# Retention over the flat row of all tokens: 36 whole chunks instead of 40 chunks with half ones

## The chip, the cores and the metric

The kernel runs on one core of a Trainium2 chip. The metric is the device time of one execution in microseconds (us); lower is better. The core has a matrix engine (TensorE, PE in the profile, with PEld for its weight loads), VectorE (DVE), ScalarE (ACT), GpSimd (POOL) and SyncE (SP), which issues most DMAs.

## The reference, cut to what matters

Two stages. The first is retention: for each of 8 sequences and 8 heads, causal scores weighted with a power of a decay, times v. The second is a feed-forward layer with a squared ReLU. All is fp32.

```python
batch, n_heads, seq, head_dim = (8, 8, 576, 64)      # q, k, v
scores = (1.0 / np.sqrt(D_)) * np.matmul(q, k.transpose(0, 1, 3, 2))
gamma = 1.0 - 2.0 ** (-5.0 - np.arange(H))
Dmat = np.where(rel >= 0, gamma[:, None, None] ** rel[None, :, :], 0.0)   # rel = i - j
x = np.matmul(scores * Dmat, v)                      # then to (4608 tokens, 512)
h = np.maximum(x @ w_in, 0.0)                        # w_in (512, 2048)
out = h * h @ w_out                                  # w_out (2048, 512)
```

A sequence has 576 tokens: four and a half times 128, or nine halves of 64. The rows of x are the tokens of sequence 0, then of sequence 1, and so on: a flat row of 4608 tokens, which is 36 times 128.

## The kernel before

**Retention in chunks.** The scores are not formed over whole sequences. Tokens are taken in chunks of 128, each of two halves of 64 (`C`, `CH`). The decay is split into a factor on q (`scale_q`, L374) and one on v (`scale_v`, L488), both from the table `dv`, so that a plain causal mask is left. For a half chunk of 64 tokens, `own_of` multiplies the masked scores with v; the influence of all earlier halves comes through a state of 64 x 64 per head, which `grow_of` sums up in PSUM (`u_ps`), `grown` copies to SBUF (`u_sb`), and TensorE multiplies with q (the loops at L518 and L645: "reads of the state"). The first half of a sequence reads no state, the last grows none. All matmuls here are 64 x 64; the two heads of a pair sit on different halves of the array.

**Chunks of a sequence.** The list `chunks` (L91) starts anew with each sequence: four chunks of 128 tokens and one of 64, 40 in all. For the half one, `cs` is 64: its instructions work on 64 of the 128 partitions, `retain_a` returns at once, and `grow_of` of its second half is left out.

**Three forms.** Chunks 0 to 3 are worked on whole (`scores_full`, `retain_full`). Chunks 4 to 9 are turned by TensorE (`turn_in`, L431) and worked on in three pieces (`retain_a`, `retain_b`, `retain_c`) between steps of the feed-forward layer. From chunk 10 on (`N_TURN` is 11, `N_ONE` 10), q and k are turned by VectorE (`flip`, L399) and moved to their place by ScalarE in 16 small copies per chunk (`move`, L414), and `whole` (L624) does one chunk's retention in one block:

```python
out_of, into = own_of(i, 0, 1), grow_of(i, 1) if more else []
m = beside_each(out_of, into, (0, 2))[-1]
...
grows = i + 1 < N_CH and chunks[i + 1][3] == C
out_of, into = own_of(i, 1, 1) if cs == C else [], grow_of(i + 1, 0) if grows else []
beside_each(out_of, into, (0, 2))
```

`beside_each` issues two own products, then two growing products, in turn: own products of one half take one half of the array's rows, growing products of the next half the other. `whole` also makes the scores of the next chunk (L472) and masks them on VectorE (`masked`, L484). `wait_for` puts a nop on TensorE that waits for an earlier matmul.

**The feed-forward layer.** It goes in 9 blocks of 512 tokens (`TOK`). Block 0's first product (`first_in`, L716, 16 steps) is computed while the weights are converted by VectorE in small pieces (`round_parts`, L212 to L230). For the other blocks, `ffn_in` makes the first product in 28 steps each, four groups of seven products (a Strassen-like scheme, `PRODUCTS`, kept in three PSUM banks h_a, h_b, h_c in the order a b c a b c b). A step is 4 matmuls (L752) and what follows on ScalarE (L762, L768), VectorE (L764, L766, L771, L775, L778, the square L759, the sums L693 and L694) or GpSimd (the square L769). The conversion of w_out (`w_out_parts`) and the sums of x (`sum_x`, L676 to L679) fill VectorE in the same steps.

**The order** is written out by hand (L894 to L993): for each chunk its block, the loads of a later one, then some steps. How many steps is set in `ffn` (L839) from the tokens gone by (`PACE`). SP issues the loads in that order (`load`, L133): two DMAs for q, two for k, one for v. When retention is over (about 507 us) the rest of the first product follows, and from 561 us on the second product (`inner`, L1094), which retention does not touch.

Of the kernel before, what the change touches and what calls it, by code (L numbers as in the profile page):

```python
# [40 lines left out]
def kernel(  # L41
# [48 lines left out]
    NCH = -(-S // C)  # L90
    chunks = [(b, ci, ci * C, min(C, S - ci * C)) for b in range(B) for ci in range(NCH)]  # L91
    N_CH = len(chunks)
# [40 lines left out]
    def load(i, names="qkv"):  # L133
        b, ci, c0, cs = chunks[i]
        if i == 0:
            nc.sync.dma_start(dv, decays)
        got = loaded.setdefault(i, [None] * 3)
        for name, pool, src in (("q", ld3, q), ("k", ld5, k), ("v", ld4, v)):
            if name not in names:
                continue  # L140
            t = got["qkv".index(name)] = pool.tile([128, H, D], F32, tag=name, name=f"{name}_ld")

            issue = nc.scalar if i == 0 and name != "q" else nc.sync
            at = src[b, :, c0:c0 + cs, :].rearrange("h s d -> s h d")
            if name == "v":
                issue.dma_start(t[:cs], at)
            else:

                for e in range(2):
                    issue.dma_start(t[:cs, e * HP:(e + 1) * HP, :], at[:, e::2, :])  # L150
# [167 lines left out]
    dv = only.tile([128, H, 2 * NCH], F32, name="dv")  # L318
# [55 lines left out]
    def scale_q(i, engine):  # L374
        ci, cs = chunks[i][1], chunks[i][3]
        t = loaded[i][0][:cs]
        engine.tensor_tensor(t, t, dv[:cs, :, NCH + ci:NCH + ci + 1].to_broadcast([cs, H, D]), op=ALU.mult)  # L377

# [3 lines left out]
    N_TURN = 11  # L382
# [11 lines left out]
    def flip(i):  # L394
        cs = chunks[i][3]
        t = work2.tile([128, 4, 2, HP, 32], F32, tag="flip", name="flip")

        def one(j):
            nc.vector.transpose(t[:cs, :, j, :, :], loaded[i][j][:cs].rearrange("s (p e) (d a) -> s (e d) p a", e=2, d=2))  # L399

        def two():
            one(0)
            to = new_qk(i)
            for b in range(cs // 32):
                for g in range(4):

                    moves.append((i, done[0] + 2, to[32 * g:32 * g + 32, :, :, 32 * b:32 * b + 32], t[32 * b:32 * b + 32, g, :, :, :]))

        flips.extend([lambda: one(1), two])
# [7 lines left out]
    def turn_in(i, js=(1, 0)):  # L417

        cs = chunks[i][3]
        n_h = cs // CH  # L420
        if "p" not in st[i]:
            if i < N_EARLY:
                p = [ps_e.tile([128, 512], F32, tag=f"e{h}", name="t_ps") for h in range(2)]
            else:
                t = ps_t[0].tile([128, 2, 512], F32, tag="t", name="t_ps")
                p = [t[:, h, :] for h in range(2)]
            st[i]["p"] = [x.rearrange("p (j d t) -> p j d t", j=2, d=HP) for x in p]
        for j in js:
            for hp in range(HP):
                for h in range(n_h):  # L430
                    nc.tensor.transpose(st[i]["p"][h][:, j, hp, :], loaded[i][j][rows(h), 2 * hp:2 * hp + 2, :],  # L431
                                        ident[rows(h), rows(h)])

    def turn_out(i, engines=(0, 1)):

        n_h = chunks[i][3] // CH
        p = st[i].pop("p")
        to = new_qk(i)
        copies = (nc.scalar.copy, nc.vector.tensor_copy)
        if n_h == 2:  # L440
            for h in range(2):
                copies[engines[h]](to[:, :, :, CH * h:CH * h + CH], p[h])
        else:
            for j in (1, 0):
                copies[1 - j](to[:, j, :, 0:CH], p[0][:, j, :, :])
# [5 lines left out]
    def scores(i, part=False):  # L451

        b_, ci, c0, cs = chunks[i]
        if i < N_EARLY:

            sc = [ps_f.tile([128, 512], F32, tag="f", name="sc_ps")[:, 0:256].rearrange("p (h t) -> p h t", h=HP) for e in range(2)]
        else:
            both = ps_t[0].tile([128, 2, 512], F32, tag="t", name="sc_ps")[:, :, 0:256].rearrange("p e (h t) -> p e h t", h=HP)
            sc = [both[:, e, :, :] for e in range(2)]
        st[i]["sc"] = sc  # L460
        st[i]["both"] = None if i < N_EARLY else both
        if part:
            return
        for hp in range(HP):
            score(i, hp)
        masked(i)

    def score(i, hp):
        for h in range(chunks[i][3] // CH):
            for e in range(2):  # L470
                t = slice(CH * h, CH * h + CH)
                nc.tensor.matmul(st[i]["sc"][e][rows(h), hp, :], lhsT=st[i]["kT"][rows(e), hp, t], rhs=st[i]["qT"][rows(e), hp, t],  # L472
                                 start=True, stop=True, skip_group_check=True)

    def masked(i):

        b_, ci, c0, cs = chunks[i]
        sc, both = st[i]["sc"], st[i]["both"]
        r = st[i]["ret"] = st[i]["kT"].rearrange("p (e a) (b t) -> p e (a b) t", e=2, b=2)
        if i < N_EARLY:  # L480
            for e in range(2):
                nc.vector.tensor_tensor(r[:cs, e, :, :], sc[e][:cs], msk[:cs, 0, :, :].to_broadcast([cs, HP, CH]), op=ALU.mult)
        else:
            nc.vector.tensor_tensor(r[:cs], both[:cs], msk[:cs].to_broadcast([cs, 2, HP, CH]), op=ALU.mult)  # L484
# [3 lines left out]
    def scale_v(i):  # L488
        ci, cs = chunks[i][1], chunks[i][3]
        vs = st[i]["vs"] = loaded[i][2]  # L490
        nc.gpsimd.tensor_tensor(vs[:cs], vs[:cs],  # L491
                                dv[:cs, :, ci:ci + 1].to_broadcast([cs, H, D]), op=ALU.mult)
# [4 lines left out]
    def grown(i, h):  # L497
        nc.scalar.copy(u_sb[(2 * chunks[i][1] + h + 1) % 3], u_ps[0])

    def retain_a(i):  # L500

        b_, ci, c0, cs = chunks[i]
        xp[0] = ps_x.tile([128, 2, 256], F32, tag="x", name="x_ps", padded_shape=[128, 2, 512])
        clean.clear()
        if cs < C:
            return
        beside_each(own_of(i, 1, 1), grow_of(i, 0), range(0, H, 2))
        grown(i, 0)

    def retain_b(i):  # L510

        s = st[i]
        b_, ci, c0, cs = chunks[i]
        for h in reversed(range(cs // CH)):
            if 2 * ci + h == 0:
                continue
            u = u_sb[(2 * ci + h) % 3]
# [5 lines left out]
    def retain_c(i):  # L523

        b_, ci, c0, cs = chunks[i]
        more = ci + 1 < NCH
        own, grow = own_of(i, 0, 0), grow_of(i, 1) if more else []
# [3 lines left out]
        x_out(i, lambda: grown(i, 1) if more else None)  # L531
# [17 lines left out]
    def carry_full(i):  # L549
# [3 lines left out]
        if chunks[i][1] == 0:  # L553
            u_ps[0] = ps_u.tile([128, HP, D], F32, tag="u", name="u_ps")
            return
        u = u_sb[2 * chunks[i][1] % 3]
# [4 lines left out]
    def retain_full(i):  # L561

        ci = chunks[i][1]
# [3 lines left out]
        for hp, e, b in HEADS:  # L567
            nc.tensor.matmul(u_ps[0][rows(e), hp, :], lhsT=loaded[i][1][:, 2 * hp + e, :], rhs=st[i]["vs"][:, head(hp, e), :],
                             start=(ci == 0 and hp == 0), stop=(hp == HP - 1), skip_group_check=True)
        x_out(i, lambda: grown(i, 1))  # L570

    def x_out(i, after):

        b_, ci, c0, cs = chunks[i]
        tok = b_ * S + c0
        at = tok
        p = xp[0][:, :, 0:256].rearrange("p a (g t) -> p a g t", g=2)
        while at < tok + cs:
            n = at // TOK

            while steps and steps[0][0] <= n - 2:
                if i >= N_ONE:
                    move(2)
                step()
            end = min(tok + cs, (n + 1) * TOK)
            nc.scalar.copy(xT[n][:, :, at - n * TOK:end - n * TOK].rearrange("p (g a) t -> p a g t", a=2),
                           p[:, :, :, at - tok:end - tok])
            if at == tok:
                after()
            at = end  # L590
            if n_next[0] < N_BLK and (n_next[0] + 1) * TOK <= at:
                steps.extend(block_steps(n_next[0]))
                n_next[0] += 1
        st[i] = loaded[i] = None


    def grow_of(i, h):

        ci = chunks[i][1]
        if ci == 0 and h == 0:  # L600
# [4 lines left out]
            start=(ci == 0 and h == 0 and hp == 0), stop=(hp == HP - 1), skip_group_check=True) for hp, e, b in HEADS]  # L605
# [18 lines left out]
    def whole(i):  # L624

        b_, ci, c0, cs = chunks[i]
# [3 lines left out]
        more = ci + 1 < NCH  # L630
        out_of, into = own_of(i, 0, 1), grow_of(i, 1) if more else []
        m = beside_each(out_of, into, (0, 2))[-1]
        beside_each(out_of, into, (4, 6))
        if more:
# [6 lines left out]
        for h in range(cs // CH):  # L641
            if 2 * ci + h == 0:
                continue
            u = u_sb[(2 * ci + h) % 3]
# [3 lines left out]
        grows = i + 1 < N_CH and chunks[i + 1][3] == C  # L648
        out_of, into = own_of(i, 1, 1) if cs == C else [], grow_of(i + 1, 0) if grows else []
# [5 lines left out]
        if cs == C:  # L655
            wait_for(m)
        beside_each(out_of, into, (4, 6))
        x_out(i, lambda: grown(i + 1, 0) if grows else None)
# [180 lines left out]
    def ffn(i, half):  # L839

        gone[0] += chunks[max(0, min(i, N_CH - 1))][3] / 2
        if half == 2:
            gone[0] += chunks[min(i + 1, N_CH - 1)][3] / 2
# [110 lines left out]
    for i in range(N_EARLY + 1, N_CH + 1):  # L954
# [9 lines left out]
        else:  # L964
# [11 lines left out]
            if i == N_ONE:  # L976
# [3 lines left out]
                grown(i, 0)  # L980
# [220 lines left out]
def _decays(B, H, S, D):  # L1201
# [4 lines left out]
    n = -(-S // C)  # L1206
    s = np.arange(n * C).reshape(n, C)
# [37 lines left out]
```

## Time and profile before

| | us |
|---|---|
| three executions | 961.95, 962.40, 962.91 (median 962.4) |
| the execution profiled | 962.51, span of its trace 960.6 |
| first retention block in one piece | from 121.07 |
| last retention block | from 506.56 |
| second product begins | about 561 |

| engine | busy share of the span from 100 to 508 us |
|---|---|
| TensorE | 404.0 of 408 us |
| VectorE | 350.1 |
| ScalarE | 255.6 |
| GpSimd | 100.6 |

In a list of groups a row names the line, the engine, the operation, what is written and read, the shape (partitions x elements) and the count, then total busy time, mean ns of one, and the engine's idle time just before them with what ended it. In a timeline a row has start and length in us. In a list of waits the numbers are total, times and longest. TensorE's records of one fp32 matmul come in twos, so that a step of 4 matmuls shows as x8.

### The profile page before, as it was taken

The numbers are of one execution on the slowest core, as the hardware profiler recorded it, in microseconds if no ns is written. First come the engines' busy times: TensorE is split into PE (matmuls) and PEld (weight loads), VectorE is DVE, ScalarE is ACT, GpSimd is POOL, SyncE is SP. The second block draws the span as 40 slices with busy tenths as digits, with TensorE's granted clock in tenths as the row PEclk, the third lists the DMA queues.
The fourth block names the chain that finished last, engine by engine and source line by source line (L and its number), as shares of the span: only waits on it lengthen the run. The fifth ranks groups of instructions, "written<-read, shape, count | busy, mean of one in ns | idle before, by whom it ended". The sixth has DMA issues, their size and how long they took to land. (4 is left out here: it accounts for less than half of the span.)

```text
span 960.6 us, 23424 instructions
## 1 busy us (share of the span) xinstructions
PE 945.7 (98%) x9750; PEld 848.6 (88%) x9750; DVE 787.7 (82%) x1446; ACT 337.3 (35%) x807; POOL 135.4 (14%) x123
## 2 busy tenths in 40 slices
PE   8999999999999999999999999999999999999998
PEld 6654788888888888888888899999999999999998
DVE  5889799879799797987966588888888787787876
ACT  3444485856756766757520010000000000000000
POOL 4312132223213213212110000000000000000000
PEclk9999999999999999999999999999999999999999
DMA  9985666767667756765259985435444454524251
GB/s 228 258 242 120 172 187 179 202 221 214 180 170 234 232 166 177 253 177 151 95 221 351 363 277 205 160 138 187 149 171 176 170 190 156 198 100 176 89 176 44
DMA packets 172778, 181.40 MB, mean 189 GB/s; under 512 B 118912, under 2 KB 133248, under 8 KB 166016
## 3 DMA queue, kind: packets, MB, share of 16 engines
q1 hardware_dynamic: 170576, 179.38, 59.5%
q8 instruction: 76, 1.25, 0.6%
q10 hardware_dynamic: 2096, 0.52, 0.2%
q14 instruction: 30, 0.25, 0.1%
HBM read 109.36 MB, written 70.52 MB: 187 GB/s over the span
## 5 line engine op out<-in xcount | busy, mean ns | idle before, releaser
L752 PE MATMUL h_b<-room,w 128*128 128x256 f32 x768 | 183.6, 382 | 2.1 <-DVE room L771 1.8
L414 ACT COPY qk<-flip 32x256 f32<-32x256 f32 x416 | 167.4, 402 | 6.1
L752 PEld LDWEIGHTS h_b<-room,w 128*128 128x128 f32 x768 | 144.1, 190 | 23.9 <-DVE room L771 3.2
L1094 PE MATMUL o_b<-w,room 128*128 128x128 f32 x1168 | 144.4, 275 | 0.2 <-DVE room L1046 0.2
L1094 PEld LDWEIGHTS o_b<-w,room 128*128 128x128 f32 x1168 | 137.3, 192 | 0.4 <-DVE room L1046 0.4
L752 PE MATMUL h_a<-room,w 128*128 128x256 f32 x512 | 122.0, 381 | 1.8 <-issue 1.8
L1094 PE MATMUL o_c<-w,room 128*128 128x128 f32 x1008 | 123.0, 275 | 0.0
L752 PE MATMUL h_c<-room,w 128*128 128x256 f32 x512 | 121.7, 380 | 0.0
L1094 PEld LDWEIGHTS o_c<-w,room 128*128 128x128 f32 x1008 | 117.7, 192 | 0.0
L752 PEld LDWEIGHTS h_a<-room,w 128*128 128x128 f32 x512 | 96.4, 190 | 15.1 <-issue 1.7
L1108 ACT COPY r<-o_a 128x128 f32<-128x128 f32 x53 | 14.1, 266 | 271.6 <-PE o_a L1094 235.9
L752 PEld LDWEIGHTS h_c<-room,w 128*128 128x128 f32 x512 | 96.7, 190 | 13.3
L1094 PE MATMUL o_a<-w,a 128*128 128x128 f32 x688 | 85.6, 275 | 0.0
L769 POOL TENSOR_TENSOR room<-room 128x512 f32<-128x512 f32 x32 | 35.9, 1121 | 335.9 <-ACT room L768 299.4
L1094 PEld LDWEIGHTS o_a<-w,a 128*128 128x128 f32 x688 | 81.2, 192 | 0.1
L759 DVE SCALAR_TENSOR_TENSOR room<-room 128x512 f32<-128x512 f32 x96 | 70.7, 736 | 3.3
L716 PE MATMUL h_ps<-room,w 128*128 128x512 f32 (+2 forms) x160 | 59.6, 518 | 3.5 <-DVE w L230 2.2
L377 POOL TENSOR_TENSOR q_ld<-q_ld,dv 128x512 f32<-128x512 f32 (+1 forms) x39 | 46.2, 1185 | 80.6 <-DMA q_ld<-in_q_dram 76.1
L491 POOL TENSOR_TENSOR v_ld<-v_ld,dv 128x512 f32<-128x512 f32 (+1 forms) x40 | 53.9, 1349 | 7.0 <-DMA v_ld<-in_v_dram 7.0
L716 PEld LDWEIGHTS h_ps<-room,w 128*128 128x128 f32 x160 | 26.8, 190 | 27.4 <-issue 20.7
L609 PEld LDWEIGHTS x_ps<-qk,v_ld 64*64 64x64 f32 x1024 | 38.8, 134 | 13.0 <-issue 11.6
L771 DVE TENSOR_TENSOR room<-h_b,room 128x512 f32<-128x512 f32 x32 | 21.9, 684 | 33.5 <-PE h_b L752 33.5
(115 smaller groups left out, 1377.1 us busy)
## 6 DMA issues: line engine op xcount, KB each, us to landing
g_dram<-room SPq DMA_DIRECT2D x164, 256.0 KB, 3.9
a<-g_dram SPq DMA_DIRECT2D x30, 1024.0 KB, 5.8
room<-g_dram SPq DMA_DIRECT2D x15, 1024.0 KB, 5.9
w<-w_dram SPq DMA_DIRECT2D x7, 1792.0 KB, 10.7
out_dram<-room SPq DMA_DIRECT2D x17, 512.0 KB, 3.3
q_ld<-in_q_dram SPq DMA_DIRECT2D x64, 128.0 KB, 4.1
w<-in_moe_w_in_dram SPq DMA_DIRECT2D x16, 512.0 KB, 6.4
w<-in_moe_w_out_dram SPq DMA_DIRECT2D x16, 512.0 KB, 4.2
```

The costliest lines, as they stand in the source:

```text
L377: engine.tensor_tensor(t, t, dv[:cs, :, NCH + ci:NCH + ci + 1].to_broadcast([cs, H, D]), op=ALU.mult)
L414: nc.scalar.copy(*moves.pop(0)[2:])
L491: nc.gpsimd.tensor_tensor(vs[:cs], vs[:cs], dv[:cs, :, ci:ci + 1].to_broadcast([cs, H, D]), op=ALU.mult)
L609: return [lambda hp=hp, e=e, b=b: nc.tensor.matmul(x_at(hp, e, b, h), lhsT=s["vs"][rows(h), head(hp, e), :], rhs=s["ret"][rows(h), e, hp, ...
L716: nc.tensor.matmul(p, lhsT=w[:, c, :], rhs=xT[0][:, c, :].rearrange("p (h t) -> p h t", h=2)[:, lo:hi, at[0]:at[1]], start=(c == 0), stop= ...
L752: nc.tensor.matmul(p[:, mm, :], lhsT=w[:, c, :], rhs=xs[n][right][:, c, :], start=(j in OPENS and mm == 0 and c == 0), stop=(j in CLOSES a ...
L759: nc.vector.scalar_tensor_tensor(t, t, 0.0, t, op0=ALU.max, op1=ALU.mult)
L769: nc.gpsimd.tensor_tensor(g["A11"], g["A11"], g["A11"], op=ALU.mult)
L771: nc.vector.tensor_tensor(g["A22"], p, p15, op=ALU.add)
L1094: nc.tensor.matmul(p, lhsT=s["lefts"][left][:, m, :], rhs=w_out[j][:, m, WO_SLOT[right], :], start=(i in OPENS and m == 0), stop=(i in CLO ...
L1108: nc.scalar.copy(r[:, 0, 0:128], p)
```

## The change

The chunks no longer start anew with a sequence. There are `n_tok // C` = 36 of them, all of 128 tokens, along the flat row; the half with number `2 * i + h` has the position `(2 * i + h) % 9` in its sequence. Two sequences take nine chunks; in the fifth of them, the first half is the end of one sequence and the second half the start of the next. Which half reads and grows a state is decided by half. The loads of such a chunk are two for each one of another chunk, with 64 rows each. The decay table has nine patterns of chunks instead of five, and goes from 80 to 144 columns. The three forms change over at chunk 9 instead of 10 (`N_TURN` 10), which is the same token. Before the reads of a state beside which no state was grown, `retain_b` waits for the products before. `x_out` no longer splits a chunk at a block's border. The diff, cut to its core:

```diff
-    NCH = -(-S // C)
-    chunks = [(b, ci, ci * C, min(C, S - ci * C)) for b in range(B) for ci in range(NCH)]
-    N_CH = len(chunks)
+    N_CH = n_tok // C
+    N_SEQ = S // CH
+    N_PAT = decays.shape[2] // 2
+
+    def pos(i, h):
+        return (2 * i + h) % N_SEQ
+
+    def grows(i, h):
+        return i < N_CH and pos(i, h) < N_SEQ - 1
...
+            b, c0 = divmod(i * C, S)
+            runs = [(b, c0, slice(0, C))] if c0 + C <= S else [(b, c0, slice(0, CH)), (b + 1, 0, slice(CH, C))]
+            for e in range(1 if name == "v" else 2):
+                for b, c0, to in runs:
...
-    dv = only.tile([128, H, 2 * NCH], F32, name="dv")
+    dv = only.tile([128, H, 2 * N_PAT], F32, name="dv")
...
-    N_TURN = 11
+    N_TURN = 10
...
-        if cs < C:
-            return
-        beside_each(own_of(i, 1, 1), grow_of(i, 0), range(0, H, 2))
-        grown(i, 0)
+        st[i]["made"] = beside_each(own_of(i, 1, 1), grow_of(i, 0), range(0, H, 2))[-1]
+        if grows(i, 0):
+            grown(i, 0)
...
-        for h in reversed(range(cs // CH)):
-            if 2 * ci + h == 0:
+        if not grows(i, 0):
+            wait_for(s["made"])
+        for h in (1, 0):
+            if pos(i, h) == 0:
                 continue
-            u = u_sb[(2 * ci + h) % 3]
+            u = u_sb[(2 * i + h) % 3]
...
-        ci = chunks[i][1]
-        if ci == 0 and h == 0:
+        if not grows(i, h):
+            return []
+        begins = pos(i, h) == 0
+        if begins:
             u_ps[0] = ps_u.tile([128, HP, D], F32, tag="u", name="u_ps")
...
-        grows = i + 1 < N_CH and chunks[i + 1][3] == C
-        out_of, into = own_of(i, 1, 1) if cs == C else [], grow_of(i + 1, 0) if grows else []
+        out_of, into = own_of(i, 1, 1), grow_of(i + 1, 0)
         beside_each(out_of, into, (0, 2))
...
-        gone[0] += chunks[max(0, min(i, N_CH - 1))][3] / 2
-        if half == 2:
-            gone[0] += chunks[min(i + 1, N_CH - 1)][3] / 2
+        gone[0] += C if half == 2 else C / 2
...
-    n = -(-S // C)
-    s = np.arange(n * C).reshape(n, C)
+    half = np.arange(2 * (S // CH)) % (S // CH)
+    s = (half[:, None] * CH + np.arange(CH)).reshape(-1, C)
```

## The prediction

> **What bounds the kernel now.** I read the engine shares first. TensorE is busy for 98% of the span; VectorE follows with 82%.
>
> ```profile
> span 960.6 us, 23424 instructions
> PE 945.7 (98%) x9750; PEld 848.6 (88%) x9750; DVE 787.7 (82%) x1446; ACT 337.3 (35%) x807; POOL 135.4 (14%) x123
> ```
>
> TensorE is the bound nearly everywhere, so a change is worth what it takes from TensorE's own sequence, or from the 15 us in which TensorE idles. The list of waits, cut to PE, says what those are:
>
> ```profile
> PE h_ps L716 <- DVE w L230: 2.2, 3, 1.6
> PE h_a L752 <- issue: 1.8, 1, 1.8
> PE h_b L752 <- DVE room L771: 1.8, 2, 1.3
> ```
>
> About 5.4 us of idle lie in the first 40 us and 2.6 at the end; the middle has these three lines: weights that VectorE converts (40 to 100 us), one idle without visible cause at 411.9, and a PSUM bank that VectorE must read before the sixth product of a step group goes into it.
>
> Next the timeline of PE around a half chunk. A feed-forward step (8 records of L752) repeats every 1.73 us; between runs of steps lie the retention matmuls (shortened with a line of dots here):
>
> ```profile
> 161.04 1.89 PE L752 MATMUL h_a<-room,w 128*128 128x256 f32 x8
> 162.86 0.27 PE L609 MATMUL x_ps<-qk,v_ld 64*64 64x64 f32 x2
> ...
> 164.88 1.99 PE L752 MATMUL h_b<-room,w 128*128 128x256 f32 x8
> ...
> 171.89 1.89 PE L752 MATMUL h_c<-room,w 128*128 128x256 f32 x8
> 173.71 0.62 PE L609 MATMUL x_ps<-qk,v_ld 64*64 64x64 f32 x13
> ```
>
> From 162.86 to 164.88 is the retention of the last full chunk of a sequence (2.02 us), five steps take 8.83, and at 173.71 the half chunk begins (1.78, to 175.49). Reading all such starts from 121 to 507 gives three prices. A full chunk costs 2.13 us. The last full chunk and the half chunk cost 2.02 + 1.78 = 3.80. A run of n steps takes 1.727 n + 0.19 (5: 8.83, 6: 10.55, 7: 12.28): 0.19 for the change between the two kinds of matmul, once a chunk.
>
> Then the groups by shape: what a half chunk costs elsewhere.
>
> ```profile
> L399 DVE STREAM_TRANSPOSE flip<-q_ld 128x512 f32<-128x512 f32 x23 | 16.1, 699 | 0.0
> L399 DVE STREAM_TRANSPOSE flip<-q_ld 64x512 f32<-64x512 f32 x6 | 4.2, 695 | 0.0
> L491 POOL TENSOR_TENSOR v_ld<-v_ld,dv 128x512 f32<-128x512 f32 x32 | 43.6, 1362 | 6.2 <-DMA v_ld<-in_v_dram 6.2
> L491 POOL TENSOR_TENSOR v_ld<-v_ld,dv 64x512 f32<-64x512 f32 x8 | 10.4, 1300 | 0.7 <-DMA v_ld<-in_v_dram 0.7
> ```
>
> Half the rows, the same time. Last, busy times per stretch, chunk by chunk (columns: length, PE, PEld, DVE, ACT, POOL with counts, clock, DMA):
>
> ```profile
> 249.74:264.15 14.41, 14.40 (x169) 12.50 (x168) 11.52 (x20) 11.43 (x25) 3.57 (x3) 1.00 0.48 140
> 264.15:278.57 14.42, 14.42 (x185) 12.63 (x184) 13.61 (x20) 8.86 (x21) 3.96 (x3) 1.00 0.54 147
> 278.57:292.99 14.42, 14.42 (x185) 12.62 (x184) 14.28 (x23) 7.25 (x17) 4.03 (x3) 1.00 0.75 212
> 409.72:425.95 16.23, 14.39 (x186) 12.70 (x185) 12.05 (x20) 8.63 (x20) 3.52 (x3) 1.00 0.48 137
> 463.55:479.57 16.02, 14.69 (x186) 12.54 (x185) 15.85 (x25) 8.85 (x21) 3.97 (x3) 1.00 0.28 101
> ```
>
> The first three are periods in which retention happens to fall between two groups of seven products, 14.42 us each with TensorE full. In the changed program's list of instructions nearly every period from chunk 9 on has this form, so the trace already holds samples of it. It also warns: VectorE is busy for 14.28 of 14.42 us in the third.
>
> **What the Trainium skill says.** "TensorE: Matmul & The Clock Gate", Part 3 (row/col tiling): small matmuls on different parts of the array run concurrently. The trace agrees: 64x64 matmuls last 0.22 us, yet 64 records of L609 and L603 with 32 scores and 32 reads of the state fit in 2.13. So 8 own products that stand alone cost about what 8 own and 8 growing products cost together. "VectorE: DVE Perf Modes", the TRN2 errata: an fp32 tensor_tensor takes (N+151)/0.96 ns by elements per partition, 691 for 512. The masking (L484) has 684 for 128 rows and 679 for 64: rows don't count. "SBUF — State Buffer", who interferes with whom: GpSimd and VectorE share a port pair under an exclusive lock. The trace agrees: while GpSimd worked from 464.4 to 468.3, L224 and L227 took 1.54 and 1.43 us; their medians are 0.68 and 0.69.
>
> **The change part by part.** 40 chunks become 36; the order around the chunks from 9 on (10 before) is the same code.
>
> *TensorE, chunk stage.* The lists hold 4957 matmul-queue instructions before and after: none is removed. What goes is the form. Before: from the first retention block of this form (121.07) to the start of the last (506.56) are 385.5 us with 183 steps. After, by the list: 26 periods, 25 with 7 steps and one with 8: 26 x 14.42 + 1.73 = 376.6 us, the same 183 steps. Difference 8.9. Of these, 4.2 are idle that before has and the model of after has not (1.9 at 411.9, 1.6 at 470.7, 0.7 at 230); 4.7 are fewer transitions (3 x 0.19 = 0.6) and pairing (the rest). The last block doubles from 0.91 to some 1.5: minus 0.6. Sure part 4.1.
>
> *TensorE, chunks 4 to 9.* Up to the last conversion (96.6 us) both lists have the same 14 first-layer steps and nearly the same retention; chunk 4 with 128 tokens adds about 0.6 (8 own products beside a turn, 1.27 instead of 0.64), which eats idle on L230 rather than time, since VectorE sets that stretch. After that, before needs 121.07 - 100.24 = 20.8 us with 9 steps, 17.4 when I take off two steps. After needs one block of about 2.0 (1.78 at 110.31, plus 8 reads of the state) and one run of 7 steps, 12.3, plus 0.3 for the wait on the sums of x that before shows at 104: 14.6. Gain 2.8.
>
> *A new wait there.* The flips of chunks 10 and 11 both come in that one run. ScalarE has 14 of chunk 10's 16 copies behind the fourth step's ReLU (ending about 7.6 us into the run): 14 x 0.41 = 5.8, to 13.4, while TensorE wants the chunk at 12.3 + 0.5. The state copy and then the reads of the state queue behind: loss 0.8, once.
>
> *VectorE.* 6 transposes, 4 maskings go: 6 x 0.70 + 4 x 0.68 = 6.9 us. GpSimd: 8 scalings of 1.2 to 1.3 go, 10 us, and with them up to 8 x 0.85 of stretched VectorE work. ScalarE loses 16 short copies of x_ps (0.37) and gains 8 long ones (0.59): 1.2 less. All lie beside TensorE's steps; they count only as fewer idles of TensorE.
>
> *Loads.* SP has 511 instructions before and after: a pair of sequences takes 50 loads either way, 10 of them with 64 rows. Chunk 4's load gets 10 DMAs for 5; at 0.6 us an issue, the w_in pieces behind it on SP leave 3 us later, with 0.4 MB ahead of them, 1.6 us at the 246 GB/s of 20 to 40 us. They were issued at 24.4 and first used at 42.9, landing takes 6.4: hidden. The decay table grows from 40 to 72 KB ahead of the first q, which everything waits for: 0.1 to 0.2 us.
>
> *The added wait* (a nop in front of the state reads where no state grows before) occurs only at chunk 4, a whole first-layer step after the matmul it waits for; 8 reads and chunk 5's scores are behind it: nothing.
>
> *Idle.* Of the 4.2 us of idle in the chunk stage I cannot price what returns: bounds 0 and, with samples like 463.55, well above. Both L771 stalls had retention or a new chunk's flips between the fourth and fifth product, which the new order never has; the idle at 411.9 is unexplained and I leave it. I take 2.5 as returning, 0.6 more for the start and crowded spots of VectorE in block 1.
>
> Sum: 4.1 + (4.2 - 2.5) + 2.8 - 0.8 - 0.6 = 7.2 us. The profiled span of 960.6 becomes 953.4; that execution was timed at 962.5, close to the median 962.4, so 955.2. The second stage (561 us on) has the same instructions.
>
> **The rivals.** *VectorE pays as well (951.5):* with 7 us less work and less locking, none of the 4.2 idle returns, and the first-layer stalls on L230 shrink. For it: 250 to 293 ran without any idle. Against it: L771 ended at 290.9 and its bank was due at 292.99 - 1.73 = 291.3.
>
> *Nothing (962.4):* TensorE has the same 4957 instructions and is 98% busy. For it: that count. Against it: 3.80 against 2.13 us, in every sequence.
>
> *Slower (964.7):* the new alignment puts GpSimd's three operations (square, two scalings, 4 us from the fourth product on) over VectorE's L771 in every period, where before it drifted. If it comes late by 0.35 us on average, 27 periods lose 9.5 us; above 0.27 each the gain is gone. For it: 0.4 us of slack at 290.9, and a conversion of 1.5 us is what such a lock costs. Against it: the three samples lost nothing.
>
> **How the numbers follow.** The forecast 0.71 (953 to 958), VectorE pays 0.16, nothing 0.05, slower 0.08. The likeliest gives 955.2. Range 951 to 961: it takes in the rival below, and loses about 13 in 100 above. A measurement of this kernel tells 0.2% (1.9 us) from no change. Faster 0.87, same 0.05, slower 0.08.
>
> **What would show it.** Right: starts of retention blocks 14.42 us apart from about 115 us on, 27 blocks of 2.1 us, the first of them at 115 or so and one small stall in it; the second stage begins 7 us earlier. Wrong: waits of PE h_b on the fifth product's addition in most periods (slower), or blocks with lone own products well over 2.13 us (no gain from pairing).

## The result, and the profile after

| | before | after |
|---|---|---|
| median, us (lowest to highest) | 962.51 (961.95 to 962.91) | 957.53 (956.79 to 958.06) |
| span of the profiled execution | 960.6 | 955.5 |

The ratio is 0.9948, with a 95% interval of 0.9931 to 0.9965: the change saves 5.0 us, between 3.3 and 6.6. The prediction was 955.2, so the direction and the range held, and the gain was 5.0 us where 7.2 were expected, which is above the interval.

The head of the page of after, to be held against the one shown of before:

```profile
span 955.5 us, 23378 instructions
PE 939.5 (98%) x9750; PEld 844.1 (88%) x9750; DVE 786.7 (82%) x1435; ACT 335.7 (35%) x798; POOL 126.0 (13%) x115
```

TensorE has the same 9750 records and 6.2 us less busy time; VectorE, at 786.7 for 787.7, seems to have gained nothing, though the groups by shape show that its work went as foreseen (52 transposes and 36 scalings of v, and no rows with 64 partitions any more):

```profile
L405 DVE STREAM_TRANSPOSE flip<-k_ld 128x512 f32<-128x512 f32 x26 | 18.2, 700 | 0.0
L405 DVE STREAM_TRANSPOSE flip<-q_ld 128x512 f32<-128x512 f32 x26 | 18.2, 699 | 0.0
L488 POOL TENSOR_TENSOR v_ld<-v_ld,dv 128x512 f32<-128x512 f32 x36 | 51.4, 1429 | 8.9 <-DMA v_ld<-in_v_dram 6.0 <-PE u_ps L560 3.0
```

Look at the mean of L488: 1429 ns, 1362 before. VectorE's operations got longer too: L231, a step of the weights' conversion, takes 841 ns on average (714 before, as L224), and the square L741 takes 765 (736 before, as L759). That eats the difference. Between 98 and 515 us, 35 operations of VectorE last over 1.05 us in after and 30 in before, every one of them while GpSimd works, although GpSimd has fewer operations. The list of waits, cut to PE, with the same lines as before and one more (L734 is the first product, L752 before; L753 the fifth product's addition, L771 before; L698 the first layer):

```profile
PE h_ps L698 <- DVE w L237: 2.6, 3, 1.2
PE h_b L734 <- DVE room L753: 1.9, 2, 1.5
PE h_a L734 <- issue: 0.7, 1, 0.7
PE sc_ps L470 <- ACT qk L420: 0.5, 1, 0.5
```

The idle without visible cause shrank from 1.8 to 0.7, the wait on the fifth product's addition is as large as before (1.9 for 1.8), and the fourth line is the predicted flush of chunk 10's moves (0.8 forecast, 0.6 of extra time in the first block).

Busy times per period of after (columns as before) show the form that was expected, and what it looks like when it fails:

```profile
248.70:263.12 14.42, 14.41 (x169) 12.51 (x169) 11.43 (x19) 11.46 (x25) 3.52 (x3) 1.00 0.70 211
263.12:277.54 14.42, 14.42 (x186) 12.63 (x185) 14.28 (x21) 8.86 (x21) 3.97 (x3) 1.00 0.70 174
131.05:147.21 16.16, 14.68 (x185) 12.54 (x184) 16.02 (x24) 8.85 (x21) 4.43 (x3) 1.00 0.54 142
```

In the second row VectorE works 14.28 of 14.42 us and TensorE still loses nothing. In the third VectorE is full (16.02 of 16.16) and TensorE loses 1.7. The timeline there (VectorE, GpSimd and TensorE; left out are TensorE's steps before):

```profile
141.12 1.51 POOL L751 TENSOR_TENSOR room<-room 128x512 f32<-128x512 f32 x1 [10.72 <-ACT room L750]
141.64 1.53 DVE L231 SCALAR_TENSOR_TENSOR w<-w,w 128x512 f32<-128x512 uint32 x1
...
142.59 1.50 POOL L384 TENSOR_TENSOR q_ld<-q_ld,dv 128x512 f32<-128x512 f32 x1
143.21 1.43 DVE L234 TENSOR_TENSOR w<-w,w 128x512 f32<-128x512 f32 x1
144.05 1.50 POOL L488 TENSOR_TENSOR v_ld<-v_ld,dv 128x512 f32<-128x512 f32 x1
144.56 0.68 DVE L753 TENSOR_TENSOR room<-h_b,room 128x512 f32<-128x512 f32 x1
...
145.29 1.99 PE L734 MATMUL h_b<-room,w 128*128 128x256 f32 x8 [1.48 <-DVE room L753]
```

Two pieces of a w_out conversion, 0.68 and 0.69 us elsewhere, take 1.53 and 1.43 beside GpSimd. L753, for which TensorE waits, stands behind them in VectorE's order.

**Where the 5.1 us of the span came from.** I cut both timelines at the same marks of TensorE, and subtracted the idle that the rows carry:

| stretch | before | after | gain |
|---|---|---|---|
| to the first block in one piece (two steps more before: 3.45) | 121.07 | 116.03 | 1.6 |
| first to last block: blocks, without idle | 29: 59.40 | 26: 54.69 | 4.7 |
| the same: runs (183 steps), without idle | 321.55 | 320.98 | 0.6 |
| the same: idle | 4.5 | 5.2 | -0.6 |
| the last block | 0.91 | 1.68 | -0.8 |
| from it to the second product (two steps more after) | 32 steps | 34 steps | -0.3 |

That is 5.1, but for rounding. "Without idle" means: a run is n x 1.727 + 0.19, and what it has above is idle; blocks are the sum of their lengths less the idle marked in them.

### The profile page after: what moved, and what is told of

Its sections match the earlier page's. It is cut to its first block, busy times and chain, and to the rows that moved or that the text cites. A ratio compares the mean times of both kernels' runs of the same rounds, so it can differ in the third digit from the quotient of the medians.

```text
span 955.5 us, 23378 instructions
## 1 busy us (share of the span) xinstructions
PE 939.5 (98%) x9750; PEld 844.1 (88%) x9750; DVE 786.7 (82%) x1435; ACT 335.7 (35%) x798; POOL 126.0 (13%) x115
## 3 DMA queue, kind: packets, MB, share of 16 engines
q8 instruction: 76, 1.25, 0.6%
## 5 line engine op out<-in xcount | busy, mean ns | idle before, releaser
L734 PE MATMUL h_b<-room,w 128*128 128x256 f32 x768 | 182.0, 380 | 2.3 <-DVE room L753 1.9
L734 PEld LDWEIGHTS h_b<-room,w 128*128 128x128 f32 x768 | 145.4, 190 | 23.5 <-DVE room L753 3.2
L734 PE MATMUL h_a<-room,w 128*128 128x256 f32 x512 | 124.0, 384 | 0.8 <-issue 0.7
L734 PE MATMUL h_c<-room,w 128*128 128x256 f32 x512 | 121.0, 379 | 0.0
L734 PEld LDWEIGHTS h_c<-room,w 128*128 128x128 f32 x512 | 97.3, 190 | 13.2
L734 PEld LDWEIGHTS h_a<-room,w 128*128 128x128 f32 x512 | 95.1, 190 | 14.8 <-issue 1.2
L741 DVE SCALAR_TENSOR_TENSOR room<-room 128x512 f32<-128x512 f32 x96 | 73.5, 765 | 3.3
L698 PE MATMUL h_ps<-room,w 128*128 128x512 f32 (+2 forms) x160 | 59.6, 518 | 4.0 <-DVE w L237 2.6
L488 POOL TENSOR_TENSOR v_ld<-v_ld,dv 128x512 f32<-128x512 f32 x36 | 51.4, 1429 | 8.9 <-DMA v_ld<-in_v_dram 6.0
L753 DVE TENSOR_TENSOR room<-h_b,room 128x512 f32<-128x512 f32 x32 | 22.0, 688 | 37.0 <-PE h_b L734 37.0
L698 PEld LDWEIGHTS h_ps<-room,w 128*128 128x128 f32 x160 | 26.8, 190 | 28.1 <-issue 20.7
L595 PE MATMUL x_ps<-qk,v_ld 64*64 64x64 f32 x1024 | 48.3, 222 | 0.0
```

What stands on the lines that cost most here:

```text
L488: nc.gpsimd.tensor_tensor(vs, vs, dv[:, :, at:at + 1].to_broadcast([C, H, D]), op=ALU.mult)
L595: return [lambda hp=hp, e=e, b=b: nc.tensor.matmul(x_at(hp, e, b, h), lhsT=s["vs"][rows(h), head(hp, e), :], rhs=s["ret"][rows(h), e, hp, ...
L698: nc.tensor.matmul(p, lhsT=w[:, c, :], rhs=xT[0][:, c, :].rearrange("p (h t) -> p h t", h=2)[:, lo:hi, at[0]:at[1]], start=(c == 0), stop= ...
L734: nc.tensor.matmul(p[:, mm, :], lhsT=w[:, c, :], rhs=xs[n][right][:, c, :], start=(j in OPENS and mm == 0 and c == 0), stop=(j in CLOSES a ...
L741: nc.vector.scalar_tensor_tensor(t, t, 0.0, t, op0=ALU.max, op1=ALU.mult)
L753: nc.vector.tensor_tensor(g["A22"], p, p15, op=ALU.add)
```

## The experiments

Two theories were to be told apart. Mine, on record: the gain is TensorE's, from fewer blocks and from own products paired with growing ones, and the relief of the other engines counts only as fewer idle stretches. The rivals: pairing is worth nothing; and the relief of VectorE and GpSimd is (a part of) the gain. Each kernel was timed against the kernel before on its own chip (962.7 to 963.0). "First to last" is the stretch of 380.83 us in after and 385.49 in before; its idle is worked out as above.

### Pairing

**All blocks unpaired** (e1):

```diff
     def beside_each(own, grow, js):
         made = []
-        for j in js:
-            made.extend(f() for f in own[j:j + 2] + grow[j:j + 2])
+        for part in (own, grow):
+            for j in js:
+                made.extend(f() for f in part[j:j + 2])
```

> The changed kernel, but each group of own products is issued before its group of growing products instead of in turn with it, everywhere after chunk 4. Theory (the gain comes from pairing own with growing products on different halves of the array): a lone group of 8 takes about what a pair of groups takes, 0.5 us, so each of some 55 pairs loses 0.42 us: 23 us slower, blocks of 3.0 us instead of 2.13. Rival (the matrix engine overlaps neighbouring groups by itself, and pairing is worth little): under 5 us slower.

Measured: 959.67 (958.48 to 960.99), ratio 0.9964 [0.9952, 0.9977]. Blocks took 2.17 instead of 2.13. TensorE's timeline in one of them shows why my theory was wrong here:

```profile
207.18 0.27 PE L595 MATMUL x_ps<-qk,v_ld 64*64 64x64 f32 x2
207.21 0.27 PE L589 MATMUL u_ps<-v_ld,k_ld 64*64 64x64 f32 x2
207.29 0.23 PE L595 MATMUL x_ps<-qk,v_ld 64*64 64x64 f32 x2
207.32 0.22 PE L589 MATMUL u_ps<-v_ld,k_ld 64*64 64x64 f32 x2
```

Four own products are issued before four growing ones, yet their records start in turn, 30 ns apart, as in after. By these starts, the order of issue over so short a distance doesn't decide whether they run side by side.

**Unpaired only in blocks where a sequence ends** (e2), with the same edit under a condition:

```diff
+        apart = pos(i, 1) == 0
-        m = beside_each(out_of, into, (0, 2))[-1]
+        m = beside_each(out_of, into, (0, 2), apart)[-1]
```

> The changed kernel, but only where the end of one sequence meets the start of the next (five places in the blocks of one piece) are own and growing products issued one group after the other. Theory of pairing: 5 x 0.42 = 2.1 us slower (959.6), all in five blocks of 2.5 us. Rival (fewer transitions and idle times make the gain): within 0.5 us of the changed kernel.

Measured: 958.25 (957.1 to 959.53), ratio 0.9955 [0.9941, 0.9969]; 0.03 to 0.04 us a block, as the rival had it.

**Growing products wholly after the own ones** in the second part of each block (e5), so that eight own products, with scores of the next chunk between them, come before eight growing ones:

```diff
-        beside_each(out_of, into, (0, 2))
+        beside_each(out_of, [], (0, 2))
...
-        beside_each(out_of, into, (4, 6))
+        beside_each(out_of, [], (4, 6))
+        beside_each([], into, (0, 2, 4, 6))
```

> The changed kernel, but in the second part of each block of one piece the growing products come after all own products instead of in turn with them, so that nothing on other rows of the array is beside them. The first run with groups of four issued apart lost only 0.04 us a block, and its trace shows own and growing products still side by side. Theory of pairing, corrected (what counts is that both lie near each other in the sequence, not that they alternate): now they don't, and 26 blocks lose 0.3 us each, 8 us (965.5). Rival (pairing is worth nothing, a block has a fixed cost of its own, and the gain is in having 27 blocks instead of 30): under 2 us.

Measured: 960.99 (959.81 to 963.65), ratio 0.9981 [0.9973, 0.9989]. Most blocks took 2.32, first to last 383.56: 2.7 us more, between the two expectations. Pairing is real and worth 0.19 us for one group of eight, less than half of the 0.42 that I took for e1. At each of the five sequence ends in this stretch, before leaves three groups alone (the own products of the last full chunk and of the half chunk, and the growing ones of the next start), and after leaves one. By e5's price the five pairs that the change forms are worth about 1 us (an estimate, 5 x 0.19) of the 4.7 that the blocks became shorter.

### The relief of VectorE and GpSimd

**All of it put back, and more** (e3): at each sequence's end the transposes, the masking and two scalings are done twice (the scalings by 1), with the same values. That is 12 transposes and 6 maskings, where the change took away 6 and 4, and 12 scalings for 8.

```diff
+            for _ in range(2 if ends(i) else 1):
                 nc.vector.transpose(t[:, :, j, :, :], loaded[i][j].rearrange("s (p e) (d a) -> s (e d) p a", e=2, d=2))
...
+            for _ in range(2 if ends(i) else 1):
                 nc.vector.tensor_tensor(r, both, msk.to_broadcast([C, 2, HP, CH]), op=ALU.mult)
...
         nc.gpsimd.tensor_tensor(vs, vs, dv[:, :, at:at + 1].to_broadcast([C, H, D]), op=ALU.mult)
+        if ends(i):
+            nc.gpsimd.tensor_tensor(vs, vs, msk[:, 0, :, CH - 1:CH].to_broadcast([C, H, D]), op=ALU.mult)
```

> The changed kernel with the work of VectorE and GpSimd put back, and more: in the last chunk of six sequences, one more masking and two more transposes (18 x 0.69 = 12.4 us of VectorE, where the change took 6.9) and two more scalings on GpSimd (12 x 1.3 us). The values stay as they are (each is written twice, or multiplied by one). Theory (both lie beside the matrix engine): within 1.5 us of the changed kernel. Rival (the freed VectorE is what pays): back by 5 us or more, to 962.5.

Measured: 973.63 (972.27 to 978.02), ratio 1.0124 [1.0103, 1.0145]: 12 us slower than the kernel before. This was the largest surprise. Work of the kind that I had put "beside TensorE's steps" costs some 16 us against after. Not all of that is waiting. The profile also gives the clock that TensorE was granted, and around the end of three of the long stalls (4.0, 2.5 and 2.6 us) it was halved, for 13.6 us in all (from 148.9, 346.9 and 480.0 us). TensorE worked in 12.4 of them, so about 6 of the 19.2 us by which first to last is longer in this profile are lost to the clock (an estimate, half of 12.4); in after it is full all through this stretch. It was also more work than the change took, so the next two put back one part each.

**VectorE's alone** (e6): 6 second transposes (of k) and 5 second maskings, 7.6 us; the change took 6.9.

```diff
+            for _ in range(2 if ends(i) and j else 1):
                 nc.vector.transpose(t[:, :, j, :, :], loaded[i][j].rearrange("s (p e) (d a) -> s (e d) p a", e=2, d=2))
...
+            for _ in range(2 if ends(i) and i > 16 else 1):
                 nc.vector.tensor_tensor(r, both, msk.to_broadcast([C, 2, HP, CH]), op=ALU.mult)
```

> The changed kernel with VectorE's work alone put back, about as much as the change took: one more transpose of k and (five times) one more masking in the last chunks of the sequences, 11 x 0.69 = 7.6 us. Putting back double the transposes together with 12 scalings lost 16 us. If VectorE's free time in a period is all used (what the last run suggests), 3 to 8 us slower; if GpSimd's lock is what did it, under 1.5 us.

Measured: 963.87 (961.93 to 968.34), ratio 1.0011 [1.0004, 1.0019]. The whole gain is gone. First to last takes 387.07, 6.2 more, of which about 4.5 is idle (9.7 for after's 5.2). The list of waits has it, under L758, which is after's L753:

```profile
PE h_b L739 <- DVE room L758: 5.6, 3, 3.2
PE h_b L739 <- DVE room L751: 1.0, 1, 1.0
```

The other 1.7 us is the clock (an estimate, half of the 3.4 us below). The longest stall, 3.22 us, ends at 150.06, and just after it TensorE is granted half its clock (PEclk is the column before the last two):

```profile
150.06 2.57 PE L739 MATMUL h_b<-room,w 128*128 128x256 f32 x8 [3.22 <-DVE room L758]
151.30:154.70 3.40, 3.40 (x84) 2.67 (x86) 3.33 (x7) 0.37 (x1) 0.00 (x0) 0.50 0.43 92
```

Of the 21 executions, 14 have a mean clock of 0.996 or 0.998. The seven at 1.0 have a median of 962.72, where before has 963.03: at full clock, too, next to nothing of the gain is left.

**GpSimd's alone** (e7): six second scalings of v, 8.4 us; the change took 8 scalings of q and v, 10 us.

```diff
         nc.gpsimd.tensor_tensor(vs, vs, dv[:, :, at:at + 1].to_broadcast([C, H, D]), op=ALU.mult)
+        if ends(i):
+            nc.gpsimd.tensor_tensor(vs, vs, msk[:, 0, :, CH - 1:CH].to_broadcast([C, H, D]), op=ALU.mult)
```

> The changed kernel with GpSimd's work alone put back: one more scaling of v (by one, 1.4 us) in the last chunks of six sequences, 8.4 us of GpSimd that nothing waits for. If the lock on VectorE is what costs, each can stretch up to two operations of VectorE by 0.85 us just ahead of the fifth product's addition: 3 to 6 us slower. If VectorE's own work is what costs, under 1.5 us.

Measured: 960.92 (960.59 to 962.53), ratio 0.9978 [0.9969, 0.9987]; first to last 382.99, 2.2 more. GpSimd is 13% busy, and still 8 us of it cost 2 to 3. TensorE does not wait for GpSimd itself, but for additions of VectorE (2.8 us in 4 waits in the place of L753, 1.9 in 2 in after).

**The other side: the kernel before, relieved** (e9). Its chunks and TensorE's list stay; the six half chunks from chunk 14 on lose their transposes on VectorE and their scalings on GpSimd (that of q under the same condition as that of v):

```diff
-            nc.vector.transpose(t[:cs, :, j, :, :], loaded[i][j][:cs].rearrange("s (p e) (d a) -> s (e d) p a", e=2, d=2))
+            (nc.vector.transpose if cs == C or i < 11 else nc.scalar.copy)(t[:cs, :, j, :, :], loaded[i][j][:cs].rearrange("s (p e) (d a) -> s (e d) p a", e=2, d=2))
...
+        if cs == C or i < 11:
+            nc.gpsimd.tensor_tensor(vs[:cs], vs[:cs],
+                                    dv[:cs, :, ci:ci + 1].to_broadcast([cs, H, D]), op=ALU.mult)
```

> The kernel before, in its 40 chunks, with the six later half chunks relieved: their 12 transposes go from VectorE (8.4 us less) to ScalarE as plain copies, and GpSimd leaves out their scalings of q and v (12 x 1.2 to 1.3 us, 15 us less). TensorE's list and the chunks stay as they were; a half chunk's q, k and v are then neither turned nor weighted. It asks whether the relief of the other engines alone is the gain. If relief alone pays, at least 2 us less than before (under 961.0). If the gain takes both (fewer TensorE transitions, and the other engines able to follow), within 1 us of before: the chunk stage of before holds only 4.2 us of idle, of which a relief can take some, and its two waits on L771 (1.8 us) are the most that I see at stake.

Measured: 960.41 (960.13 to 961.1), ratio 0.9974 [0.9963, 0.9984]: 2.5 us faster, with no change of the chunks. First to last 383.03 for 385.49, blocks and steps as before, idle 2.3 for 4.5 (five blocks also took 2.08 for 2.13). Its two lines that answer to those of before:

```profile
PE h_a L754 <- issue: 1.3, 1, 1.3
PE h_b L754 <- DVE room L773: 0.4, 1, 0.4
```

The wait on the fifth product's addition fell from 1.8 to 0.4: the stall of 1.33 at 470.7 is gone. Another 0.5 came from the idle that the waits call "issue", which is not explained. VectorE has 20 operations over 1.05 us between 98 and 515 us here, where before has 30. I had expected at most 1 us, so the rival held: relief pays by itself. But this relief (8.4 us of VectorE, 15 of GpSimd) is larger than the change's (6.9 and 10), so it is no measure of what the change's own share pays.

### Where the idle of after lies

**Sums of x not begun in the first layer** (e4):

```diff
-            if n_next[0] > 1:
-                if 1 not in sums_x:
-                    sums_x[1] = sum_x(1)
-                sums_x[1].pop(0)()
```

> The changed kernel, but the sums of x for block 1 are not begun in the last steps of the first layer of block 0 (where the new order brought them, since 1024 tokens are through earlier); all four are made at block 1's first step, as before the change. Theory (two of these sums, 0.7 us each, stand in front of the last conversion that the matrix engine waits for): that step starts 1.4 us earlier, at 96.7, block 1 then waits 0.3 to 0.6 us for its sums; 0.9 us faster in all (956.6). Rival (the delay is GpSimd's lock on VectorE at 94 to 97 us): no change.

Measured: 956.98 (956.3 to 958.84), ratio 0.9945 [0.9932, 0.9957]. The step before the last of the first layer is followed by the last after 5.40 us, 6.13 in after, and block 1's first run takes 12.43 for 12.28. One sum, not two, had come ahead of the last conversion: 0.6 us net, seen in the trace but below what the times resolve.

**q scaled ahead of a period's steps** (e8), so that GpSimd does it before it has the square and the scaling of v:

```diff
+            for j in range(n_scaled[0], min(i + 4, N_CH)):
+                n_scaled[0] += 1
+                scale_q(j, nc.gpsimd)
             ffn(i - 1, 2)
```

> The changed kernel, but the scaling of a later q is issued on GpSimd before the steps of a period instead of after them, so that it no longer stands behind the square of the fourth product and runs at the period's start, away from the fifth product's addition. If the lock ahead of that addition makes the idle that is left (1.5 us at 145, 0.7 at 460 and others, in all some 3), 2 us faster (955.5). If not, no change.

Measured: 956.40 (955.83 to 956.83), ratio 0.993 [0.9917, 0.9943]; first to last 379.37, 1.5 less. The stall in the period at 452 is gone, those at 133 and 221 stay.

**Four stalls out** (e10): that, the sums as in e4, and

```diff
-                    moves.append((i, done[0] + 2, to[32 * g:32 * g + 32, :, :, 32 * b:32 * b + 32], t[32 * b:32 * b + 32, g, :, :, :]))
+                    moves.append((i, done[0] + (1 if i == N_TURN else 2), to[32 * g:32 * g + 32, :, :, 32 * b:32 * b + 32], t[32 * b:32 * b + 32, g, :, :, :]))
...
-        for _ in range(0 if busy[0] else 2 if late_w2 > 1.5 and j in (0, 3) else late_w2 > 0):
+        for _ in range(0 if busy[0] or n == 1 and j in (2, 3) else 2 if late_w2 > 1.5 and j in (0, 3) else late_w2 > 0):
```

> The kernel after, with the four stalls that I can place taken out: GpSimd scales q before a period's steps (3 us at 221, 409 and 452 in part), the sums of x of block 1 begin only when that block does, chunk 10's moves may start a step earlier (the flush of 0.5 in the first block), and no piece of w_out is converted in the third and fourth step of a block-1 group (the stall of 1.75 at 133). If the idle of the chunk stage is placed rightly, 1.5 (as measured alone) + 1.7 + 0.5 and some of 0.6: 954 us, at most 955. If the stalls only move, 956 to 957.5, like scaling first alone.

**Three stalls out** (e11): the same without the edit of e4.

> As the one before, but the sums of x of block 1 begin in the first layer as in the kernel after. If one sum before the last conversion costs what its own experiment showed, 0.5 us more than that one; if that was chance between executions, the same within 0.3.

Measured: e10 955.24 (954.38 to 957.53), e11 956.05 (954.83 to 956.34), both with a ratio of 0.9924 [0.9912, 0.9936]. First to last is 378.36 in both, 2.5 less than in after. The first block no longer waits for moves and the period at 133 no longer stalls; 2.7 us of idle are left. The early sums make no difference that these times can tell. These are the fastest kernels of the study, some 7 us below before. e10 fell a little short of its 954 to 955: in the run of steps that begins at 410.18, 1.5 us is idle, mostly without visible cause, where after had 0.3.

**Three stalls out, and VectorE's work put back** (e12), the edit of e6 on e11. It asks whether VectorE's work costs by its amount or by where it falls.

> The kernel with three stalls out (q scaled ahead of a period's steps, chunk 10's moves a step earlier, no w_out piece in two steps of block 1), and the 7.6 us of VectorE work of the earlier experiment put back (a second transpose of k at each sequence's end and a second masking, same values). There the work cost 5.9 us on the kernel after, nearly all of it in five periods where a stretched conversion or square stood before the fifth product's addition. If the amount of VectorE work sets the cost, it costs 5 to 6 us here too: 961 to 962. If it costs only where it falls on GpSimd's scalings and a conversion, the order with q scaled early should let it pass for less than 2 us: 956 to 958. My own guess lies between, nearer the second.

Measured: 959.66 (958.29 to 961.43), ratio 0.9972 [0.9964, 0.9981], 3.9 us above e11 when each is taken against its own measurement of before; first to last 382.14, 3.8 more. Neither expectation held; it came out between them, as I had guessed, but not nearer the second. In that stretch the work costs 6.2 us on after, 4.5 of them idle and 1.7 the clock, and 3.8 with the three stalls out, where the clock stayed full in the execution profiled. So the better order kept the clock from falling and took 0.7 us off the idle: most of the work's price stayed, and the better order did not remove it.

## Why the prediction was right, and which terms were mis-sized

**Right in size, and in mechanism only in part.** "4.7 are fewer transitions (3 x 0.19 = 0.6) and pairing (the rest)": measured 5.3 (4.7 for the blocks, 0.6 for the runs). I called it pairing, and by e5's price pairing is about 1 us of it. The rest goes with the number of blocks: 29 blocks of 2.05 on average become 26 of 2.10, for nearly the same tokens (64 more fall to the last block). No run changed the number of blocks by itself, so that a block has a cost of its own is argued, not shown. The size held because it was read off whole periods of before, 14.42 us each, and did not depend on the reason given; that the wrong reason did no harm is luck. Where no state grows in one half the block is not longer, as feared for own products that stand alone, but shorter: 2.01 to 2.02. Periods of 14.42 from the first block on, 27 blocks, the first at 116, one small stall in it (0.6 for 0.8), a last block that doubles (0.77 for 0.6): all seen.

**Mis-sized: "I take 2.5 as returning, 0.6 more for the start and crowded spots".** With the flush of 0.8 that allows 3.9 us of idle in the chunk stage. Measured 5.2. The two old places went (the idle at 411.9, and L771 before retention), as argued, but others came: 1.75 at 133, 1.25 at 452, 0.86 at 221. Those at 133 and 452 come from GpSimd's scaling and w_out's conversion falling together ahead of the fifth product: the one at 452 went when q was scaled earlier (e8), the one at 133 when pieces of w_out were moved as well (e11, which also lets chunk 10's moves start earlier). This is the slower rival's mechanism; it struck twice in 26 periods and not in each. The one at 221 is another: TensorE stops within the first step of the run, GpSimd does nothing from 219 to 227, and the waits call it "issue" (0.69). It stays in e8 and is gone in e11, and why is not known. In e11 0.8 comes up at 163, and the idle at 410 grows from 0.3 to 1.5.

**Mis-sized in principle: "All lie beside TensorE's steps; they count only as fewer idles of TensorE."** True as a sentence, but the price that I gave it, 4.2 - 2.5 = 1.7, supposed that idle can only shrink from before's. It depends on how full VectorE is and on what stands in its order. I also let "up to 8 x 0.85 of stretched VectorE work" go with the eight scalings; the operations over 1.05 us rose from 30 to 35 instead. e11 has 35 as well and less idle, so what counts is where they fall. In first-to-last idle, us:

| | VectorE's and GpSimd's load of before | VectorE's alone | relieved |
|---|---|---|---|
| 40 chunks | 4.5 (before) | | 2.3 (e9) |
| 36 chunks | | 9.7, and 1.7 lost to the clock (e6) | 5.2 (after) |
| 36 chunks, three stalls out | | 6.5 (e12) | 2.7 (e11) |

TensorE's sequence becomes 5.3 us shorter, and the same VectorE work then fits worse. The regrouping without the relief of VectorE would have been no gain (e6: 0.1% slower than before); the relief without the regrouping gives 2.5 us (e9); both give 5.0. So the gain does not look like a sum of a TensorE part and a rest. The put-back operations are not those that were removed and stand at other places, and e9 relieves more than the change does, which limits the reading of both to their size.

**Mis-sized: 2.8 for chunks 4 to 9; measured 1.6.** From the end of the first layer on, the gain is 3.1 us (17.4 become 14.3), a little over the forecast. What is missing lies ahead of it, where I had put nothing: the last step of the first layer begins at 98.10, at 96.61 in before. Of these 1.5 us, 0.7 is the sum of x that now comes ahead of the last conversion (e4; block 1 of x is complete after chunk 7). The other 0.8 lies in the steps before. e9, whose first layer is that of before, has its last step at 97.39 and its first block at 121.95, 0.9 later than before's own profile. On the other side, kernels with after's code up to there have their first block at 116.12 (e2), 117.40 (e7) and 118.40 (e5), and after's own 116.03 is the earliest. So this part is within what executions of the same code differ by: one pair of profiles gives 1.6, the earliest and latest of them would give anything from -0.8 to 2.5.

**The rivals.** "Nothing" is out by the interval. "VectorE pays as well" had the right resource and the wrong sign of its effect: idle did not fall to nothing, it rose by 0.6 in spite of the relief. "Slower" had the right place, L753 behind stretched work, and came in 2 periods where it needed most of them to lose the gain.

**Nothing at the end** was predicted; 0.3 was lost in the 34 steps to the second product. I did not pursue it.

**Not settled.** The idle at about 411 that the waits call "issue" is in before (1.8), e9, e10 and e11 (1.3) and e12 (2.1), at the same place in time but for different steps, and nearly absent in after. In e11 it stands where the DMA engines are over 90% busy (nearly all of 405 to 412) and where one packet of a queue of instructions is moved between 407 and 411; three more such packets up to 427 pass without idle. What it is was not tried.

## What to carry to other kernels

When one engine is 98% busy and the next 82%, a change that shortens the first one's sequence must also be priced for the second: its work per period, and what stands in its order ahead of the operation for which the first waits. Look for the period in which both are full (14.28 of 14.42 here), and put a GpSimd operation that can go early where no VectorE operation that it stretches is due. To learn whether work that disappears mattered, put it back on the new kernel and also take it off the old one: the two answers differed here, and together they suggest that the parts don't add. Before calling a difference idle, look at the granted clock of the same stretch: here some long stalls brought a halved clock, and part of what looked like waiting was that.

## What the runs showed of the hardware that was not expected

Around the end of some long stalls of TensorE its granted clock fell to 0.50 and stayed there for 3.4 us or more: with a stall of 3.22 us in e6 (from 151.3), and with 4.03, 2.45 and 2.60 in e3 (from 148.9, 346.9 and 480.0; 6.8, 3.4 and 3.4 us). It did not follow the length alone: another stall of 2.45 in e3, at 283.7, had no such stretch behind it, while in the first layer of e6 and e10 one of 1.9, at about 49, had one. What decides it was not tried.

TensorE runs own and growing 64x64 products side by side although they are issued four and four (starts 30 ns apart in e1). "TensorE: Matmul & The Clock Gate", Part 3 of the Trainium skill, says that matmuls start and end strictly in program order and that only weight loads are pulled ahead; the starts recorded in e1 differ from that, and the measured order stands.

GpSimd at 13% is no spare engine: 8.4 us more of it cost 2 to 3 us of TensorE's time (e7). At 141 to 145 us in after, the stretched operations were conversions with two SBUF inputs (1.53 and 1.43, 0.68 and 0.69 elsewhere); an addition that reads PSUM did not stretch (L753 at 144.56 took 0.68 beside L488). That agrees with "SBUF — State Buffer", Who interferes with whom, which says that a VectorE instruction with two SBUF inputs contends with a GpSimd instruction that reads SBUF. An operation with one SBUF input stretched too: L219, a conversion step, took 1.28 at 347.96 beside L488, where it mostly takes 0.42.

The first stage varies from execution to execution: the step of the first layer that begins at 49.4 in the profile of after begins at 51.0 in e4's and 50.9 in e11's, with the same code up to there, and part of the delay stays in what follows. A profile is compared between marks, and a difference under some 2.5 us in its first stage is left to the times.
